# A decode step with attention and a Mish branch: dense input product in the first unit, division behind two key pieces, w2 in the key ring, output sum in four column groups

## Chip, cores and metric

The kernel runs on one core of one Trainium2 chip. The metric is the device time of one execution in microseconds (us). 1 MB is 10^6 bytes here.

## The reference

A decode step for two sequences: attention over the last 4096 positions of a long key/value cache, a dense branch with the Mish activation, and the input itself are added.

```python
def _A_ref(x, k_cache, v_cache, wq, wo):     # x (2, 1, 448)
    W = 4096                                  # of 32768 positions; Hq 16, Hkv 8, Dh 256
    q = (x @ wq).reshape(B, Sq, Hq, Dh).transpose(0, 2, 1, 3)
    k = repeat(k_cache[:, :, Sk - W:, :], 2, axis=1)
    v = repeat(v_cache[:, :, Sk - W:, :], 2, axis=1)
    p = softmax(einsum("bhqd,bhkd->bhqk", q, k) * Dh ** -0.5)
    o = einsum("bhqk,bhkd->bhqd", p, v)
    return o.transpose(0, 2, 1, 3).reshape(B, Sq, Hq * Dh) @ wo

def _B_ref(x, w1, b1, w2):                    # w1 (448, 1792), w2 (1792, 448)
    h = einsum("bsd,df->bsf", x, w1) + b1
    return einsum("bsf,fd->bsd", h * tanh(softplus(h)), w2)

xn = layernorm(x)
return x + _A_ref(xn, ...) + _B_ref(xn, ...)
```

All inputs are bf16. Keys and values of the window are 33.6 MB each, wq and wo 3.67 MB each, w1 and w2 1.606 MB each.

## The kernel before

The 16 pairs of batch and key head are worked in four units (U = 4) of four pairs. A unit reads its keys in four pieces and its values in four pieces of 2.097 MB each, every one a tile of 128 partitions by 16,384 bytes, and its rows of wo in two loads of 0.459 MB.

All large loads go out on SP's queue, in the order in which the program names them, and a load whose buffer is still in use holds up all loads behind it. The buffers are two rings: `k_pool` with three buffers for key pieces, and `v_pool` with four, in which value pieces, the two parts of wq, w1 and the three parts of w2 take turns. wo has two buffers. The order of the work on each engine is that of the program (`manual_schedule`).

A unit runs like this. `turn(u, r, i)` (L216) transposes half a key piece on VectorE into `kt[i]`; eight of them make a unit's keys. `scores(u, i)` forms a half of the scores on PE: one product with a mask (L273), then 128 products of 128x128 weights (L284), and ScalarE takes the exponential (L292). `weigh(u)` sums the exponentials with products by ones (L304), and VectorE reduces the sum (L312) and takes its reciprocal. `values(u, g)` makes 64 products with value piece g (L325). `finish(u)` divides by the sum on VectorE (L337). `mix(u)` multiplies by wo with eight products of 448 columns (L351), which add to `psA`, a 2x448 accumulator; it stands behind the next unit's `weigh`.

Around them, `project()` (L238) makes the queries behind the first two key pieces. `dense_in()` stands at the end of the first unit: 196 products (L376) with 64 columns of w1 each, in turn for the upper and the lower half of the output partitions, then the Mish operations on VectorE and ScalarE (L385 to L403). w1 itself is loaded (L364) behind the second key piece of unit 1. `dense_out(part)` (L418) adds the 14 products with w2 to `psA`, in parts of 8, 5 and 1; w2's loads (L411) stand behind the first values of the last unit. At the end VectorE copies `psA` (L470) and one DMA writes it out (L471).

```python
    for u in range(U):
        ...                                   # turns, project, loads of v
        values(u, 0) ... values(u, 2)
        if not last:
            load_k(u + 1, 0); load_k(u + 1, 1)
            if u == 0:
                load_w1()
            load_k(u + 1, 2); load_wo(u); load_k(u + 1, 3)
        values(u, 3)
        finish(u)
        if u == 0:
            dense_in()
    dense_out(0); mix(U - 1); dense_out(1); dense_out(2)
```

Of the kernel before, what the change touches and what calls it, by code (L numbers as in the profile page):

```python
# [17 lines left out]
def kernel(  # L18
# [13 lines left out]
    nc = tc.nc  # L32
# [23 lines left out]
    HW = HqDh // 2  # L56
    NCH = HW // P
    F2 = F // 2
    NI = F // P
    assert Sq == 1 and Bsz == 2 and rep == 2 and Dh == 256 and Hq == 16  # L60
    assert W == 4096 and D == 448 and F == 1792
    scale = float(Dh) ** -0.5

# [19 lines left out]
    def ring(name):  # L83
        return v_pool.tile([P, KE], BF16, tag="v", name=name)
# [3 lines left out]
    def load_k(u, r):  # L88
        t = k_pool.tile([P, KE], BF16, tag="k", name="k")
        src = kview[u][:, s0:, :].rearrange("j (c t) d -> c j (t d)", c=C)  # L90
        nc.sync.dma_start(out=t[:], in_=src[:, :, r * KE : (r + 1) * KE])  # L91
        k_t[u, r] = t

    def load_v(u, g):
        t = ring("v")
        src = vview[u][:, s0:, :].rearrange("j (g x t) d -> g x j (t d)", g=G, x=C)
        nc.sync.dma_start(out=t[:], in_=src[g])
        v_t[u, g] = t

    def load_wo(u):  # L100
        w = wo_pool.tile([P, KU, rep, 2 * D], BF16, tag="wo", name="wo")
# [81 lines left out]
    for odd in range(2):  # L183
# [12 lines left out]
    nc.tensor.matmul(  # L196
        psA[:, :],
        lhsT=ident[0:Bsz, 0:Bsz],
        rhs=x_bf[:],
        start=True,  # L200
        stop=False,
        skip_group_check=True,
    )

    kt = [
        kt_pool.tile([P, TH * NB, P // (R * J), R, J], FP32, name=f"kt{i}") for i in range(NH)
# [139 lines left out]
    def mix(u):  # L346
        oT, w = state.pop(("oT", u)), wo_t.pop(u)
        for k2 in range(KU):
            for h in range(rep):
                for c in range(2):  # L350
                    nc.tensor.matmul(  # L351
                        psA[:, :],
                        lhsT=oT[:, c, k2 * rep + h, :],
                        rhs=w[:, k2, h, c * D : (c + 1) * D],
                        start=False,
                        stop=False,
                        skip_group_check=True,
                    )

    act_bf = consts.tile([P, NI, Bsz], BF16)  # L360

    def load_w1():
        t = ring("w1")
        nc.sync.dma_start(  # L364
            out=t[:, 0 : NS * F2], in_=B_w1.flatten().rearrange("(p e) -> p e", p=P)
        )
        state["w1"] = t

    def dense_in():
        w1 = state.pop("w1")  # L370
        w1_v = w1[:, 0 : NS * F2].rearrange("p (s q i) -> p s i q", s=NS, i=NI)
        h_ps = ps_m.tile([P, NI, Bsz], FP32, tag="m", name="h_ps")
        for i in range(NI):
            for s in range(NS):
                for k in range(2):
                    nc.tensor.matmul(  # L376
                        h_ps[k * 64 : (k + 1) * 64, i, :],
                        lhsT=w1_v[:, s, i, :],
                        rhs=xs[:, s, k, :],
                        start=(s == 0),  # L380
                        stop=(s == NS - 1),
                        skip_group_check=True,
                    )
        h_sb = consts.tile([P, NI, Bsz], FP32, name="h_sb")
        nc.vector.tensor_tensor(  # L385
            out=h_sb[:],
            in0=h_ps[:],
            in1=b1_sb[:].unsqueeze(2).to_broadcast([P, NI, Bsz]),
            op=ALU.add,
        )  # L390
        u_sb = consts.tile([P, NI, Bsz], FP32, name="u_sb")
        nc.scalar.activation(out=u_sb[:], in_=h_sb[:], func=ACT.Exp)
        t_sb = consts.tile([P, NI, Bsz], FP32, name="t_sb")
# [3 lines left out]
        den = consts.tile([P, NI, Bsz], FP32, name="den_sb")  # L397
# [9 lines left out]
    def load_w2():  # L407
        w2_in = B_w2.flatten().rearrange("(p e) -> p e", p=P)
        for lo, hi in w2_parts:
            t = ring("w2")  # L410
            nc.sync.dma_start(out=t[:, 0 : (hi - lo) * D], in_=w2_in[:, lo * D : hi * D])  # L411
            state["w2", lo] = t

    def dense_out(part):
        lo, hi = w2_parts[part]
        t = state.pop(("w2", lo))
        for i in range(lo, hi):
            nc.tensor.matmul(  # L418
                psA[:, :],
                lhsT=act_bf[:, i, :],  # L420
                rhs=t[:, (i - lo) * D : (i - lo + 1) * D],
                start=False,
                stop=(i == NI - 1),
                skip_group_check=True,
            )

    for u in range(U):
        if u == 0:
            load_k(0, 3)
        for r in range(R):  # L430
            for i in range(NH):
                turn(u, r, i)
            if u == 0 and r == 1:
                project()
# [10 lines left out]
        load_v(u, 2)  # L445
        load_v(u, 3)
        values(u, 0)
        if last:
            load_w2()
        values(u, 1)  # L450
        values(u, 2)
        if not last:
            load_k(u + 1, 0)
            load_k(u + 1, 1)
            if u == 0:
                load_w1()
            load_k(u + 1, 2)
            load_wo(u)
            load_k(u + 1, 3)
        values(u, 3)  # L460
        finish(u)
        if u == 0:
            dense_in()
    dense_out(0)
    mix(U - 1)
    dense_out(1)
    dense_out(2)

    res = consts.tile([Bsz, D], BF16)
    nc.vector.tensor_copy(out=res[:], in_=psA[:, :])  # L470
    nc.sync.dma_start(out=out.flatten_outer_dims(), in_=res[:])  # L471


# [28 lines left out]
```

## Time and profile before

| what | value |
|---|---|
| median of 3 runs | 213.32 us (213.04 to 213.45) |
| profiled execution, its own time | 212.86 us |
| profiled execution, span from first to last instruction | 211.1 us |
| PE busy | 93.2 us (44% of the span) |
| VectorE (DVE) busy | 83.5 us (40%) |
| ScalarE (ACT) busy | 7.9 us (4%) |
| mean read rate over the span | 368 GB/s |
| DMA on the chain that ended last | 56% |

Times in the rows are microseconds from the span's first instruction. PE is TensorE's products, PEld its weight loads, DVE is VectorE, SPq the instructions of SP that issue DMAs. A name such as `kt<-k` is what an instruction writes and reads. An idle time in square brackets stands before the instruction, with what ended it. "issue" means that the engine waited for nothing that the profile shows. The granted clock is that of TensorE; 1.00 is 2.4 GHz and 0.50 is 1.2 GHz.

### The profile page before, as it was taken

Reading aid. Unit: us, or ns where it says so; the run is one execution under the profiler, and the core shown is the slowest. Engines: PE = TensorE matmul, PEld = TensorE weight load, DVE = VectorE, ACT = ScalarE, POOL = GpSimd, SP = SyncE. Lnnn points to the kernel's source line nnn. Section 1 sums busy time; section 2 is a strip of 40 time slices with the busy share of each in tenths; the row PEclk is TensorE's granted clock in tenths of the full one; section 3 lists DMA queues with packets and bytes.
Section 4 is the critical chain, followed back from the end, with each engine's and each line's share of the span. In section 5 each row is a group of like instructions: output and inputs, shape, how many; then the busy total and the mean of one; then the engine's idle time right before and its main releaser. Section 6 shows DMA issues by size and latency. Waiting matters only on the chain.

```text
span 211.1 us, 5109 instructions
## 1 busy us (share of the span) xinstructions
PE 93.2 (44%) x2434; PEld 76.3 (36%) x2434; DVE 83.5 (40%) x81; ACT 7.9 (4%) x12; POOL 2.7 (1%) x12
## 2 busy tenths in 40 slices
PE   0203402966304980008792400079952000959794
PEld 0103302856304970007572300066751000845741
DVE  5693369110000019994010698531003995501001
ACT  5000000110000000001100000011000000110000
POOL 5000000000000000000000000000000000000000
PEclk9999999985555555555695555557855555587559
DMA  5999999999999500899999999999999999999920
GB/s 215 432 425 428 435 422 432 428 422 422 432 414 437 220 0 0 335 416 435 435 418 422 435 395 438 435 416 425 432 419 422 409 419 411 438 419 419 333 90 2
DMA packets 7821, 78.00 MB, mean 370 GB/s; under 512 B 884, under 2 KB 3064, under 8 KB 3320
## 3 DMA queue, kind: packets, MB, share of 16 engines
q1 hardware_dynamic: 7652, 77.66, 88.0%
q8 instruction: 19, 0.31, 0.6%
q10 hardware_dynamic: 148, 0.01, 0.0%
q14 instruction: 2, 0.02, 0.0%
HBM read 77.67 MB, written 0.00 MB: 368 GB/s over the span
## 4 chain that ended last, share of the span: by engine, by line
DMA 56%; PE 22%; DVE 16%; issue 4%; ACT 1%; SPq 0%; ACTq 0%
DMA k<-in_A_k_cache_dram 19%; DMA wo<-in_A_wo_dram 15%; DVE kt L216 15%; DMA v<-in_A_v_cache_dram 13%; DMA w<-in_B_w_dram 9%; PE sc L284 7%; PE h_ps L376 6%; PE o L325 5%; PE psA L418 2%; PE psA L351 2%; ACT p L292 1%; PE dn L304 0%; PE sc L273 0%; DVE res L470 0%; SPq L91 0%
## 5 line engine op out<-in xcount | busy, mean ns | idle before, releaser
L216 DVE STREAM_TRANSPOSE kt<-k 128x2048 f32<-128x2048 f32 x32 | 71.3, 2282 | 9.8 <-DMA k<-in_A_k_cache_dram 9.8
L284 PE MATMUL sc<-qd,kt 128*128 128x32 bf16 x1024 | 29.0, 185 | 70.4 <-DVE kt L216 63.7
L284 PEld LDWEIGHTS <-kt 128*128 128x128 bf16 x1024 | 28.0, 102 | 73.9 <-DVE kt L216 65.7
L325 PE MATMUL o<-p,v 128*128 128x8 bf16 x1024 | 28.8, 167 | 14.6 <-issue 13.0
L325 PEld LDWEIGHTS <-v 128*128 128x128 bf16 x1024 | 27.8, 101 | 17.2 <-issue 15.4
L337 DVE TENSOR_TENSOR oT<-o,rec 128x16 bf16<-128x16 f32 x4 | 0.7, 175 | 46.2 <-PE o L325 46.2
L312 DVE TENSOR_REDUCE rec<-dn 128x8 f32<-128x512 f32 x4 | 2.8, 691 | 33.0 <-PE dn L304 33.0
L376 PE MATMUL h_ps<-xs,w 128*64 128x2 bf16 x196 | 11.6, 255 | 9.0 <-DMA w<-in_B_w_dram 9.0
L376 PEld LDWEIGHTS <-w 128*64 128x64 bf16 x196 | 11.5, 212 | 9.1 <-DMA w<-in_B_w_dram 9.1
L292 ACT ACTIVATE p<-sc 128x512 bf16<-128x512 f32 x8 | 4.8, 597 | 147.4 <-PE sc L284 147.4
L351 PE MATMUL psA<-wo,oT 128*2 128x448 bf16 x32 | 9.5, 452 | 0.2 <-issue 0.2
L238 PE MATMUL q_ps<-xs,wq 128*128 128x4 bf16 x112 | 3.3, 166 | 13.3 <-DMA wq<-in_A_wq_dram 13.3
L385 DVE TENSOR_TENSOR h_sb<-h_ps,b_sb 128x28 f32<-128x28 f32 x1 | 0.2, 189 | 20.4 <-PE h_ps L376 20.4
L238 PEld LDWEIGHTS <-wq 128*128 128x128 bf16 x112 | 3.1, 104 | 13.8 <-DMA wq<-in_A_wq_dram 13.8
L351 PEld LDWEIGHTS <-oT 128*2 128x2 bf16 x32 | 3.1, 103 | 9.3 <-issue 8.4
L273 PE MATMUL sc<-mneg,ident 128*128 128x512 bf16 x8 | 4.6, 575 | 0.0
L418 PE MATMUL psA<-w,act_bf 128*2 128x448 bf16 x14 | 4.4, 480 | 0.0
L304 PE MATMUL dn<-p,ones 128*128 128x512 bf16 x8 | 3.6, 455 | 1.8 <-ACT p L292 1.8
L179 PE MATMUL xr_ps<-ident,xrow 2*128 2x2 bf16 x7 | 1.0, 181 | 5.4 <-DVE xrow L178 5.4
L470 DVE CAST res<-psA 2x448 bf16<-2x448 f32 x1 | 0.6, 610 | 6.4 <-PE psA L418 6.4
L179 PEld LDWEIGHTS <-xrow 2*128 2x128 bf16 x7 | 0.7, 99 | 5.6 <-DVE xrow L178 5.4
L250 DVE CAST qT<-q_ps 128x16 bf16<-128x16 f32 x4 | 0.4, 167 | 5.6 <-PE q_ps L238 5.6
(39 smaller groups left out, 18.1 us busy)
## 6 DMA issues: line engine op xcount, KB each, us to landing
k<-in_A_k_cache_dram SPq DMA_DIRECT2D x16, 2048.0 KB, 25.0
v<-in_A_v_cache_dram SPq DMA_DIRECT2D x16, 2048.0 KB, 22.9
wo<-in_A_wo_dram SPq DMA_DIRECT2D x8, 448.0 KB, 30.8
wq<-in_A_wq_dram SPq DMA_DIRECT2D x1, 2048.0 KB, 16.2
w<-in_B_w_dram SPq DMA_DIRECT2D x1, 1568.0 KB, 18.7
wq<-in_A_wq_dram SPq DMA_DIRECT2D x1, 1536.0 KB, 19.2
w<-in_B_w_dram SPq DMA_DIRECT2D x1, 896.0 KB, 6.7
w<-in_B_w_dram SPq DMA_DIRECT2D x1, 560.0 KB, 6.5
```

What stands on the lines that cost most here:

```text
L179: nc.tensor.transpose(xr_ps[:, s, :], xrow[:].rearrange("b a o -> b (a o)"), ident[0:Bsz, 0:Bsz])
L216: nc.vector.transpose(out=kt[i][:, :, :, r, :], in_=t[:, i * w : (i + 1) * w].bitcast(FP32).rearrange("p (a c j) -> p a c j", c=P // (R * ...
L238: nc.tensor.matmul(q_ps[:, c, :, :].rearrange("p k b -> p (k b)"), lhsT=wq_t[s][:, c * P : (c + 1) * P], rhs=xs_m[s], start=(s == 0 and c ...
L273: nc.tensor.matmul(sc[:].rearrange("p t q -> p (t q)"), lhsT=ident[:], rhs=mneg[:].rearrange("p a j h -> p (a j h)"), start=True, stop=Fal ...
L284: nc.tensor.matmul(sc[:, t, :], lhsT=ktm[i][:, t, n, e, :], rhs=qd[:, u, 2 * n + e, :, :].rearrange("p g q -> p (g q)"), start=False, stop ...
L292: nc.scalar.activation(out=p_t[i][:].rearrange("p t g q -> p (t g q)"), in_=sc[:].rearrange("p t q -> p (t q)"), func=ACT.Exp, scale=scale,)
L304: nc.tensor.matmul(dn[:].rearrange("p a q -> p (a q)"), lhsT=ones[:], rhs=p_t[i][:].rearrange("p t g q -> p (t g q)"), start=(i == 0), sto ...
L312: nc.vector.tensor_reduce(out=rec[:], in_=dn[:].rearrange("p a q -> p q a"), axis=AXIS.X, op=ALU.add)
L325: nc.tensor.matmul(po[:, c, :], lhsT=vv[:, t, c, :], rhs=p_t[t // TH][:, t % TH, g, :], start=(g == 0 and t == 0 and c == 0), stop=(g == G ...
L351: nc.tensor.matmul(psA[:, :], lhsT=oT[:, c, k2 * rep + h, :], rhs=w[:, k2, h, c * D : (c + 1) * D], start=False, stop=False, skip_group_ch ...
L376: nc.tensor.matmul(h_ps[k * 64 : (k + 1) * 64, i, :], lhsT=w1_v[:, s, i, :], rhs=xs[:, s, k, :], start=(s == 0), stop=(s == NS - 1), skip_ ...
L418: nc.tensor.matmul(psA[:, :], lhsT=act_bf[:, i, :], rhs=t[:, (i - lo) * D : (i - lo + 1) * D], start=False, stop=(i == NI - 1), skip_group ...
```

## The change

Four things are changed together.

- `dense_in` moves into the first unit, behind `project` and the third key piece's turns; w1 is loaded ahead of the first unit's fourth key piece. w1, b1 and w2 are laid out in two halves, so that `dense_in` is 49 products with 128 columns of w1 and 4 moving columns. The Mish operations become `mish()`, behind the fourth piece's turns.
- `finish(u)`, the division, stands behind the turns of the next unit's first two key pieces. The loads of a unit all stand ahead of its scores.
- w2 goes into one buffer of the key ring, in three loads: its first half behind v(3,1), and five and two blocks of its second half behind the last value piece. The last value piece comes in two loads, of 24 and 8 positions of 32. `dense_out(0)` stands ahead of the last `values`.
- The accumulator `acc` is 128x112: the 448 output columns are cut into four groups, each at another 32 partitions, so every product of 448 columns becomes four of 112 (`add_rows`). The copy at the end is 128x112, and two DMAs on two queues write the result.

```diff
-    NI = F // P
+    NI = F2 // P
+    DG = D // G
...
-    def load_v(u, g):
-        t = ring("v")
+    def load_v(u, g, lo=0, hi=T):
+        if lo == 0:
+            v_t[u, g] = ring("v")
+        t = v_t[u, g]
...
-    b1_sb = consts.tile([P, NI], BF16)
-    nc.scalar.dma_start(out=b1_sb[:, :], in_=B_b1.rearrange("(q c) -> q c", q=P))
+    b1_sb = consts.tile([P, 2, NI], BF16)
+    nc.scalar.dma_start(out=b1_sb[:], in_=B_b1.rearrange("(k q c) -> q k c", k=2, q=P))
...
-    psA = ps_a.tile([Bsz, D], FP32)
...
+    acc = ps_a.tile([P, DG], FP32)
+    for g in range(G):
+        nc.tensor.matmul(
+            acc[32 * g : 32 * (g + 1), :],
+            lhsT=ident[0:Bsz, 0:32],
+            rhs=x_bf[:, g * DG : (g + 1) * DG],
...
+    def add_rows(lhsT, rows, stop=False):
+        for g in range(G):
+            nc.tensor.matmul(
+                acc[32 * g : 32 * g + Bsz, :],
+                lhsT=lhsT,
+                rhs=rows[:, g * DG : (g + 1) * DG],
+                start=False,
+                stop=stop,
+                skip_group_check=True,
+            )
...
         for i in range(NI):
             for s in range(NS):
-                for k in range(2):
-                    nc.tensor.matmul(
-                        h_ps[k * 64 : (k + 1) * 64, i, :],
-                        lhsT=w1_v[:, s, i, :],
-                        rhs=xs[:, s, k, :],
...
+                nc.tensor.matmul(
+                    h_ps[:, i, :, :].rearrange("p k b -> p (k b)"),
+                    lhsT=w1_v[:, s, i, :],
+                    rhs=xs_m[s],
...
-    w2_parts = [(0, 8), (8, 13), (13, NI)]
...
+    w2_parts = ((0, 0, NI), (1, 0, 5), (1, 5, NI))
+
+    def load_w2(part):
+        if part == 0:
+            state["w2"] = k_pool.tile([P, KE], BF16, tag="k", name="w2")
...
+    load_w1()
+    load_k(0, 3)
+    turns(0, 0)
+    turns(0, 1)
+    project()
+    turns(0, 2)
+    dense_in()
+    turns(0, 3)
+    mish()
     for u in range(U):
...
         last = u == U - 1
         if last:
             load_wo(u)
         load_v(u, 0)
         load_v(u, 1)
+        if last:
+            load_w2(0)
+        load_v(u, 2)
+        if last:
+            load_v(u, 3, 0, 24)
+            load_v(u, 3, 24, T)
+            load_w2(1)
+            load_w2(2)
+        else:
+            load_v(u, 3)
+            load_k(u + 1, 0)
+            load_k(u + 1, 1)
+            load_k(u + 1, 2)
+            load_wo(u)
+            load_k(u + 1, 3)
         scores(u, 0)
         scores(u, 1)
         weigh(u)
         if u > 0:
             mix(u - 1)
...
+        for g in range(G):
+            if last and g == G - 1:
+                dense_out(0)
+            values(u, g)
         if not last:
...
+            turns(u + 1, 0)
+            turns(u + 1, 1)
+            finish(u)
+            turns(u + 1, 2)
+            turns(u + 1, 3)
+    finish(U - 1)
     mix(U - 1)
     dense_out(1)
     dense_out(2)
...
+    res = consts.tile([P, DG], BF16)
+    nc.vector.tensor_copy(out=res[:], in_=acc[:])
...
+    nc.sync.dma_start(out=out_v[0], in_=res_v[0])
+    nc.scalar.dma_start(out=out_v[1], in_=res_v[1])
```

## Rows read from the trace of the kernel before

**Rows 1.** The page: GB/s in 40 equal slices, bytes read, instruction fetches.
```profile
GB/s 215 432 425 428 435 422 432 428 422 422 432 414 437 220 0 0 335 416 435 435 418 422 435 395 438 435 416 425 432 419 422 409 419 411 438 419 419 333 90 2
...
q8 instruction: 19, 0.31, 0.6%
...
HBM read 77.67 MB, written 0.00 MB: 368 GB/s over the span
```

**Rows 2.** SP's timeline: start us, us, engine, line, load, count.
```profile
48.76 1.10 SPq L104 DMA_DIRECT2D wo<-in_A_wo_dram  x2
84.08 0.54 SPq L91 DMA_DIRECT2D k<-in_A_k_cache_dram  x1
...
194.89 3.65 SPq L411 DMA_DIRECT2D w<-in_B_w_dram  x3
```

**Rows 3.** The chain that ended last: start us, us, what.
```profile
47.57 18.71 DMA w<-in_B_w_dram
...
66.32 11.61 PE h_ps L376 x196
...
79.64 15.39 DVE kt L216 x7
```

**Rows 4.** VectorE's timeline: start us, us, operation, count, idle time and its end.
```profile
8.48 4.50 DVE L216 STREAM_TRANSPOSE kt<-k 128x2048 f32<-128x2048 f32 x2 [1.46 <-DMA k<-in_A_k_cache_dram]
...
28.21 4.50 DVE L216 STREAM_TRANSPOSE kt<-k 128x2048 f32<-128x2048 f32 x2 [2.16 <-DMA k<-in_A_k_cache_dram]
33.11 4.51 DVE L216 STREAM_TRANSPOSE kt<-k 128x2048 f32<-128x2048 f32 x2 [0.39 <-DMA k<-in_A_k_cache_dram]
...
127.17 4.50 DVE L216 STREAM_TRANSPOSE kt<-k 128x2048 f32<-128x2048 f32 x2 [0.28 <-DMA k<-in_A_k_cache_dram]
...
177.56 4.51 DVE L216 STREAM_TRANSPOSE kt<-k 128x2048 f32<-128x2048 f32 x2 [2.46 <-DMA k<-in_A_k_cache_dram]
190.42 0.69 DVE L312 TENSOR_REDUCE rec<-dn 128x8 f32<-128x512 f32 x1 [8.36 <-PE dn L304]
```

**Rows 5.** PE's timeline: values of unit 2, and the last values and sums.
```profile
155.59 3.58 PE L325 MATMUL o<-p,v 128*128 128x8 bf16 x128 [2.51 <-issue]
161.51 0.19 PE L325 MATMUL o<-p,v 128*128 128x8 bf16 x1 [2.35 <-issue]
...
199.51 1.52 PE L325 MATMUL o<-p,v 128*128 128x8 bf16 x51 [1.34 <-DMA v<-in_A_v_cache_dram]
...
201.67 3.15 PE L418 MATMUL psA<-w,act_bf 128*2 128x448 bf16 x8
204.61 2.56 PE L351 MATMUL psA<-wo,oT 128*2 128x448 bf16 x8
207.00 1.30 PE L418 MATMUL psA<-w,act_bf 128*2 128x448 bf16 x6
```

**Rows 6.** The timeline of all engines from 206 us on: copy and output.
```profile
208.34 0.61 DVE L470 CAST res<-psA 2x448 bf16<-2x448 f32 x1 [6.41 <-PE psA L418]
208.98 0.33 SPq L471 DMA_DIRECT2D out_dram<-res  x1
```

**Rows 7.** Groups by line and shape: busy us, mean ns of one, idle before.
```profile
L325 PE MATMUL o<-p,v 128*128 128x8 bf16 x1024 | 28.8, 167 | 14.6 <-issue 13.0 <-DMA v<-in_A_v_cache_dram 1.5
...
L325 PEld LDWEIGHTS <-v 128*128 128x128 bf16 x1024 | 27.8, 101 | 17.2 <-issue 15.4 <-DMA v<-in_A_v_cache_dram 1.7
L376 PE MATMUL h_ps<-xs,w 128*64 128x2 bf16 x196 | 11.6, 255 | 9.0 <-DMA w<-in_B_w_dram 9.0
...
L264 DVE CAST qd<-qr_ps 32x256 bf16<-32x256 f32 x4 | 1.7, 420 | 0.5 <-PE qr_ps L254 0.5
...
L250 DVE CAST qT<-q_ps 128x16 bf16<-128x16 f32 x4 | 0.4, 167 | 5.6 <-PE q_ps L238 5.6
```

**Rows 8.** Busy times and granted clock in two stretches of the last sums.
```profile
201.70:204.60 2.90, 2.90 (x9) 0.95 (x9) 0.17 (x1) 0.00 (x0) 0.00 (x0) 0.50 0.14 47
206.50:208.30 1.80, 1.80 (x10) 0.61 (x8) 0.00 (x0) 0.00 (x0) 0.00 (x0) 1.00 0.00 0
```

More of the change, by code (lines that the diff above doesn't have):

```diff
@@ L58 @@
     F2 = F // 2
-    NI = F // P
-    assert Sq == 1 and Bsz == 2 and rep == 2 and Dh == 256 and Hq == 16
+    NI = F2 // P
+    DG = D // G
+    assert Sq == 1 and Bsz == 2 and rep == 2 and Dh == 256 and G * DG == D and Hq == 16
     assert W == 4096 and D == 448 and F == 1792
@@ L92, in load_k @@
         k_t[u, r] = t
-    def load_v(u, g):
-        t = ring("v")
+    def load_v(u, g, lo=0, hi=T):
+        if lo == 0:
+            v_t[u, g] = ring("v")
+        t = v_t[u, g]
         src = vview[u][:, s0:, :].rearrange("j (g x t) d -> g x j (t d)", g=G, x=C)
-        nc.sync.dma_start(out=t[:], in_=src[g])
-        v_t[u, g] = t
+        nc.sync.dma_start(
+            out=t[:, lo * Dh : hi * Dh], in_=src[g, :, :, lo * Dh : hi * Dh]
+        )
     def load_wo(u):
@@ L193 @@
     xs_m = [xs[:, s, :, :].rearrange("p a b -> p (a b)") for s in range(NS)]
-    psA = ps_a.tile([Bsz, D], FP32)
-    nc.tensor.matmul(
[L197 to L203, printed above, removed]
+    acc = ps_a.tile([P, DG], FP32)
[4 more added lines that the diff above has]
+            rhs=x_bf[:, g * DG : (g + 1) * DG],
+            start=True,
+            stop=False,
+            skip_group_check=True,
+        )
+    def add_rows(lhsT, rows, stop=False):
[6 more added lines that the diff above has]
+                stop=stop,
+                skip_group_check=True,
+            )
     kt = [
@@ L350, in mix @@
                 for c in range(2):
[L351 to L360, printed above, removed]
+                    add_rows(oT[:, c, k2 * rep + h, :], w[:, k2, h, c * D : (c + 1) * D])
+    act_bf = consts.tile([P, NI, 2, Bsz], BF16)
     def load_w1():
@@ L371, in dense_in, with mish @@
         w1_v = w1[:, 0 : NS * F2].rearrange("p (s q i) -> p s i q", s=NS, i=NI)
-        h_ps = ps_m.tile([P, NI, Bsz], FP32, tag="m", name="h_ps")
+        h_ps = ps_m.tile([P, NI, 2, Bsz], FP32, tag="m", name="h_ps")
         for i in range(NI):
             for s in range(NS):
-                for k in range(2):
-                    nc.tensor.matmul(
-                        h_ps[k * 64 : (k + 1) * 64, i, :],
-                        lhsT=w1_v[:, s, i, :],
-                        rhs=xs[:, s, k, :],
[L380 to L384, printed above, removed]
+                nc.tensor.matmul(
+                    h_ps[:, i, :, :].rearrange("p k b -> p (k b)"),
+                    lhsT=w1_v[:, s, i, :],
+                    rhs=xs_m[s],
+                    start=(s == 0),
+                    stop=(s == NS - 1),
+                    skip_group_check=True,
+                )
+        state["h"] = h_ps
+    def mish():
+        h_ps = state.pop("h")
+        shape = [P, NI, 2, Bsz]
+        h_sb = consts.tile(shape, FP32, name="h_sb")
         nc.vector.tensor_tensor(
@@ L387, in dense_in @@
             in0=h_ps[:],
-            in1=b1_sb[:].unsqueeze(2).to_broadcast([P, NI, Bsz]),
+            in1=b1_sb[:].rearrange("p k i -> p i k").unsqueeze(3).to_broadcast(shape),
             op=ALU.add,
         )
-        u_sb = consts.tile([P, NI, Bsz], FP32, name="u_sb")
+        u_sb = consts.tile(shape, FP32, name="u_sb")
         nc.scalar.activation(out=u_sb[:], in_=h_sb[:], func=ACT.Exp)
-        t_sb = consts.tile([P, NI, Bsz], FP32, name="t_sb")
+        t_sb = consts.tile(shape, FP32, name="t_sb")
         nc.vector.scalar_tensor_tensor(
@@ L396, in dense_in @@
         )
-        den = consts.tile([P, NI, Bsz], FP32, name="den_sb")
+        den = consts.tile(shape, FP32, name="den_sb")
         nc.vector.tensor_scalar(
@@ L403, in dense_in, with turns @@
         nc.vector.tensor_tensor(out=act_bf[:], in0=h_sb[:], in1=t_sb[:], op=ALU.mult)
-    w2_parts = [(0, 8), (8, 13), (13, NI)]
[L407 to L412, printed above, removed]
+    w2_parts = ((0, 0, NI), (1, 0, 5), (1, 5, NI))
+    def load_w2(part):
+        if part == 0:
+            state["w2"] = k_pool.tile([P, KE], BF16, tag="k", name="w2")
+        k, lo, hi = w2_parts[part]
+        w2_in = B_w2.flatten().rearrange("(k p e) -> k p e", k=2, p=P)
+        at = k * NI * D
+        nc.sync.dma_start(
+            out=state["w2"][:, at + lo * D : at + hi * D],
+            in_=w2_in[k, :, lo * D : hi * D],
+        )
     def dense_out(part):
-        lo, hi = w2_parts[part]
-        t = state.pop(("w2", lo))
+        k, lo, hi = w2_parts[part]
         for i in range(lo, hi):
[L418 to L424, printed above, removed]
-            )
-    for u in range(U):
[L428 to L434, printed above, removed]
+            at = (k * NI + i) * D
+            add_rows(
+                act_bf[:, i, k, :], state["w2"][:, at : at + D], stop=(k == 1 and i == NI - 1)
+            )
+    def turns(u, r):
+        for i in range(NH):
+            turn(u, r, i)
+    load_w1()
[7 more added lines that the diff above has]
+    mish()
+    for u in range(U):
         last = u == U - 1
@@ L467 @@
     dense_out(2)
-    res = consts.tile([Bsz, D], BF16)
-    nc.vector.tensor_copy(out=res[:], in_=psA[:, :])
-    nc.sync.dma_start(out=out.flatten_outer_dims(), in_=res[:])
+    res = consts.tile([P, DG], BF16)
+    nc.vector.tensor_copy(out=res[:], in_=acc[:])
+    out_v = out.flatten_outer_dims().rearrange("b (g c) -> b g c", g=G)
+    res_v = res[:].rearrange("(g r) c -> r g c", g=G)
+    nc.sync.dma_start(out=out_v[0], in_=res_v[0])
+    nc.scalar.dma_start(out=out_v[1], in_=res_v[1])
 _INS = ['A_x', 'A_k_cache', 'A_v_cache', 'A_wq', 'A_wo', 'B_x', 'B_w1', 'B_b1', 'B_w2']
```

19 lines of the change are left out of this document (removed).

## The prediction

> **What bounds the kernel now.** I read the slices of the page first, because a decode step that has 77.67 MB to read can end no earlier than its reads. The DMA rate stands near 425 GB/s in nearly every slice and falls in two places only: slices 13 to 16 (220, 0, 0, 335 GB/s) and the last three [rows 1]. The first hole, counted against 425 GB/s, is (205 + 425 + 425 + 90)/425 = 2.7 slices of 5.28 us, 14 us. The SP timeline tells why the queue ran dry: after w1 (L364), one key piece (L91) and the wo pieces (L104) were issued from 47.57 to 49.9 us, the next load, again L91, goes out at 84.08 [rows 2, 3]. The chain of waits fills in the rest: dense_in (L376) runs on PE from 66.32 for 11.61 us as soon as w1 is there, the Mish operations follow it on VectorE, and only then, at 79.64, the seven transposes that were queued behind them [rows 3]. The load at 84.08 wanted the buffer of the piece that the first two of these turn (2 x 2.2 us = 4.4).
>
> The second place is the end. Landings can be read off the rows in which an engine's idle time ended with a DMA: the first piece at 8.48, w1 at 66.32, the last key piece at 177.56, the last value piece at 199.51 [rows 3 to 5]. After that w2 (1.606 MB) still has to come, 1.606/0.427 = 3.8 us, to about 203.3; PE works until 208.3, the copy takes 0.61, and the output leaves at 208.98 [rows 5, 6].
>
> **The stream's own rate.** From 8.48 to 66.32 us there landed k, wq, k, k, four v, two k, w1: 9 x 2.097 + 3.670 + 1.606 = 24.15 MB in 57.84 us, 417.5 GB/s. From 127.17 to 199.51 there landed 13 pieces of 2.097 and six wo pieces of 0.459 MB, 30.02 MB in 72.34 us, 415 GB/s [rows 3 to 5]. Together 416. The stretch with the fewest breaks, 33.11 to 66.32 (14.19 MB), gives 427. I take 416: an unbroken stream of 181 us has the small breaks of both stretches.
>
> **The change part by part.** *w1 and dense_in in the first unit.* w1 is issued ahead of the fourth key piece, in a third buffer of the v ring that waits for nothing; the loads behind it on SP land 1.606/0.427 = 3.8 us later, and are themselves no shorter or longer. dense_in goes from 196 products of 64 columns (11.6 us, 59 ns each [rows 3]) to 49 of 128. A full load and product of 128x128 takes 28.8/1024 = 28 ns [rows 7]; the columns here lie 7 elements apart, so I bound it by 28 and 2 x 59 ns: 1.4 to 5.8 us. It starts when w1 lands, about 28.2 + 3.8 = 32 us by the first unit's third key piece, and the next thing PE has is the scores after a key piece that lands near 37: hidden either way. On SP the load of v(0,3) waits for it, until 34 to 38, with k and three v, 8.4 MB or 20 us, still queued. The Mish operations come after all transposes of the first unit, where VectorE waited 8 us for PE anyway (as before the reduce at 190.42 [rows 4]). Cost zero; the hole goes.
>
> *Is there a new hole?* The tightest wait left on SP is the same one as before: the fourth key piece of the next unit needs its first one turned. When that first one has landed, two key pieces and two wo pieces are still queued: 5.11 MB, 12.3 us, against two transposes of 2.25 us [rows 4]. 7.8 us of cover remain. The other loads wait for values or turns of a piece that landed at least two loads earlier. So the last byte lands at 8.48 + (77.67 - 2.10)/0.416 = 190.1 us, instead of 203.3. With 427 it would be 185.5.
>
> *Division behind two key pieces.* Four transposes (9 us) go ahead of it on VectorE. Who waits: the next mix and the next unit's first values, both behind the next unit's scores, over 10 us later. In the last unit nothing is put ahead of it. Zero; it keeps the turns, and so SP's key loads, from waiting for values(u, 3).
>
> *w2 in the key ring, last v piece cut in two.* Before, its three loads waited for values of the last unit (194.89 on [rows 2]); now they wait for turns that end some 20 us before the queue reaches them. Counting back from 190.1 at 416 GB/s: last v part 188.2, its first 24 rows 186.9, v(3,2) 183.1, last key piece 163.9. The b1 load, 256 short runs instead of 128, lies ahead of ScalarE's first table load; what follows from that on VectorE ended 1.46 us before the first key piece was there [rows 4]: zero.
>
> *Sum in four column groups.* Each of 448 columns becomes four of 112. The old one paces at (204.61 - 201.67)/8 = 0.37 us at a granted clock of 0.50, 1.2 GHz, and at most 1.30/6 = 0.22 at 1.00, 2.4 GHz [rows 5, 8]. Nothing in the trace runs four column groups. From below: four issues at 28 ns, 0.11 us. From above: the same columns one after the other, 0.37. Beyond that, rival 2. I take 0.125, since at 1.2 GHz 112 columns are a quarter of 0.37, 0.09, which hides under the four issues, and since L376 already changes between two column halves with every product at 59 ns spacing with 255 ns each, so several are in flight [rows 3, 7]. For the same thing the Trainium skill (TensorE: Matmul & The Clock Gate, Part 3: Packing small matmuls) gives 2.38 times for three column tiles; by that a set would be about 0.37/2.38 = 0.155 us, an estimate, and my sum 0.45 us later. No run here shows it yet.
>
> **The sum, in the span of the profiled run.** Key piece 163.9. From the last key landing to the end of the second dn product took 177.56 to 190.4 = 12.8 before, where the reduce follows at once [rows 4], with one instruction-fetch gap in it: 176.7. mix(2), eight sets, 1.0: 177.7. values(3,0) and (3,1), 128 products at 28 ns: 181.3. There a second gap of about 2.4 us is likely: PE's instructions come in 19 packets of 16 KB [rows 1], 128 products each, and under a full DMA queue a run of products goes 128 per 5.9 us (155.59 to 161.51, gaps of 2.4) [rows 5]. v(3,2) lands at 183.1, so values(3,2) end at 185 to 186, dense_out(0) (seven sets, 0.9) at 186 to 186.8. Then PE waits for data: last v part 188.2, 16 products 0.45, division with its hand-overs 0.25, mix(3) 1.0, five sets 0.65, and the last two after 190.1: 190.8. The copy is of 128x112 instead of 2x448; rows of 16 and 256 elements take 167 and 420 ns, so about 0.27 [rows 7]: 191.1. From the old copy's end, 208.95, to the end of the span 2.14 [rows 6], and the two output DMAs go out side by side on SP and ScalarE: 193.2, against 211.1. The profiled run took 212.86, 1.76 more than its span: 195.0. It lies 0.46 under the median of 213.32, so I predict 195.5.
>
> **The rivals.** *1. Groups run one after the other.* Then a set costs 0.37 as now. mix(2) +2.0 and dense_out(0) +1.7 come ahead of the last v part and eat the spare 0.1 to 0.9 us of PE; after it come 64 products of values(3,3) that no longer hid, 1.8, mix(3) 3.0, seven sets 2.6. End of PE 195.0 to 198.0, as far as the fetch gap hides under the longer sets; time 199.7 to 202.7. For it: no row shows overlap of long products. Against: the spacing of L376. Chance 0.17.
>
> *2. Slower: changing the column group stops the array.* If a product in another group may start only when the one before is out, each of the 28 + 60 in the tail and the 32 of mix(2) costs its own duration instead of 0.03 us. By L376 that is 0.255 for 2 columns, with 110 more at 1.2 GHz 0.34; 120 x 0.31 = 37 us, time about 232. It turns the sign from (211.1 - 193.2)/120 + 0.03 = 0.18 us a product on. Against it: L376 changes halves at 59 ns, and the weight loads of L325, all on 128 rows, add up to 1024 x 101 ns = 103 us in 27.8 us of busy time, under running products [rows 7]. Chance 0.04. The Trainium skill speaks for this one (same page, Part 3, The mechanism): weight loads overlap running products only where the row groups differ, and all four groups here use all rows. By that rule the time would be that of this rival; the trace disagrees for whole-array loads, as just said, and does not show it for groups of 32.
>
> *3. The pieces of a tile wait for each other.* If dense_out(0) waits for all three w2 loads, which are parts of one tile, then 190.1 + 0.9 + 1.8 + 0.25 + 1.0 + 0.9 = 195, time 199.7. Against: the second wo load into one tile went out with the first, two in 1.10 us [rows 2]. With it I count a hole that merely moves. Together 0.08.
>
> *4. Faster:* the stream keeps 427 and PE keeps up: 190.8 to 192.5. 0.06.
>
> **How the numbers follow.** My forecast, 193 to 198, has 0.65. With rival 1, most of 3 and the edge of 4 the range 192.5 to 202.5 holds a little over 8 in 10; its lower end is the faster rate, its upper end rival 1. Faster than 213.32 by over 0.2%, about what a measurement of this kernel can tell from no change, are all but rival 2 and the worst of 3: 0.95; same 0.01; slower 0.04.
>
> **What would show it.** No slice under 400 GB/s between the first and the last two; no L91 issue that comes after its queue has emptied; last key piece turned from about 164; v(3,3)'s products waiting for DMA, not issue; a set of four at 0.11 to 0.16 us. It is wrong if PE has no wait for v in the last unit (then instruction fetch or the groups bind), if a set takes 0.3 or more, or if a new stretch without data appears.

## The result and the profile after

| | before | after |
|---|---|---|
| median | 213.18 us | 198.03 us (197.72 to 198.26) |
| ratio to before, 95% interval | | 0.929 (0.927 to 0.932) |
| profiled execution | 212.86 us | 197.72 us |
| its span | 211.1 us | 195.2 us |

The forecast was 195.5 us, in a range of 192.5 to 202.5. The page of the changed kernel: the span, the read rate in 40 slices (of 4.88 us now) and the packets in which instructions were fetched.

```profile
span 195.2 us, 5096 instructions
...
GB/s 215 396 427 425 434 430 429 430 430 423 423 423 430 423 408 430 430 423 426 426 423 426 396 433 426 426 426 430 426 423 420 397 421 421 430 416 420 394 140 2
...
q8 instruction: 18, 0.29, 0.6%
```

The slices of 220, 0, 0 and 335 GB/s [rows 1] have no counterpart. From the second slice to the 38th the rate never falls under 394. The forecast had named 400 as the mark; four slices lie between 394 and 397, none of them a stretch without data. The median lies 0.03 us above the band of 193 to 198 that the forecast put first.

SP's timeline, start us, us, line, load, count. The last of these loads stood 84 us into the old run [rows 2].

```profile
35.57 6.55 SPq L92 DMA_DIRECT2D k<-in_A_k_cache_dram  x3
42.18 1.10 SPq L108 DMA_DIRECT2D wo<-in_A_wo_dram  x2
66.04 0.54 SPq L92 DMA_DIRECT2D k<-in_A_k_cache_dram  x1
```

The fourth key load of unit 1 now goes out at 66.04, some 7.7 us before the queue would be empty. VectorE's timeline (idle time and what ended it in brackets) shows the landings of the last unit's key piece and of one in mid-run.

```profile
103.28 4.50 DVE L232 STREAM_TRANSPOSE kt<-k 128x2048 f32<-128x2048 f32 x2 [11.17 <-DMA k<-in_A_k_cache_dram]
109.46 4.50 DVE L232 STREAM_TRANSPOSE kt<-k 128x2048 f32<-128x2048 f32 x2 [1.67 <-DMA k<-in_A_k_cache_dram]
114.45 4.51 DVE L232 STREAM_TRANSPOSE kt<-k 128x2048 f32<-128x2048 f32 x2 [0.43 <-DMA k<-in_A_k_cache_dram]
...
163.26 4.50 DVE L232 STREAM_TRANSPOSE kt<-k 128x2048 f32<-128x2048 f32 x2 [2.84 <-DMA k<-in_A_k_cache_dram]
```

VectorE waits for keys before every pair of transposes; before, it worked through a backlog. The last key piece is there at 163.26, 14.3 us earlier than at 177.56 [rows 4].

PE's timeline of the first dense product and of the end. L212 is the sum in four groups, L341 values, L300 scores.

```profile
32.18 2.77 PE L384 MATMUL h_ps<-xs,w 128*128 128x4 bf16 x49 [7.67 <-DMA w<-in_B_w_dram]
...
173.56 1.04 PE L300 MATMUL sc<-qd,kt 128*128 128x32 bf16 x35 [1.68 <-issue]
...
175.65 0.56 PE L212 MATMUL acc<-wo,oT 128*2 128x112 bf16 x32
176.15 1.63 PE L341 MATMUL o<-p,v 128*128 128x8 bf16 x59
179.75 2.00 PE L341 MATMUL o<-p,v 128*128 128x8 bf16 x69 [1.98 <-issue]
182.46 1.73 PE L341 MATMUL o<-p,v 128*128 128x8 bf16 x59 [0.70 <-DMA v<-in_A_v_cache_dram]
185.95 0.30 PE L341 MATMUL o<-p,v 128*128 128x8 bf16 x5 [1.76 <-issue]
186.18 0.82 PE L212 MATMUL acc<-w,act_bf 128*2 128x112 bf16 x28
187.41 1.87 PE L341 MATMUL o<-p,v 128*128 128x8 bf16 x64 [0.41 <-DMA v<-in_A_v_cache_dram]
189.55 1.20 PE L212 MATMUL acc<-wo,oT 128*2 128x112 bf16 x32 [0.27 <-DVE oT L353]
190.50 0.90 PE L212 MATMUL acc<-w,act_bf 128*2 128x112 bf16 x28
```

From the last key piece on, PE stops for "issue" after every 128 products (35 + 2 + 32 + 59, then 69 + 59), three times some 1.8 us, and twice for a value piece. The trace has the starts of the instruction packets, too: 171.12, 177.37 and 183.54 us. PE goes on 2.4 us after each, at 173.56, 179.75 and 185.95, so these stops are waits for instructions. The end, all engines:

```profile
191.44 0.28 DVE L494 CAST res<-acc 128x112 bf16<-128x112 f32 x1 [1.95 <-PE acc L212]
191.74 0.67 SPq L497 DMA_DIRECT2D out_dram<-res  x1
191.75 0.58 ACTq L498 DMA_DIRECT2D out_dram<-res  x1
```

From the copy's end at 191.72 to the end of the span it is 3.5 us; before it was 2.1 [rows 6].

### The profile page after: what moved, and what is told of

It is laid out like the page before. It is cut to its first block, busy times and chain, and to the rows that moved or that the text cites. A ratio compares the mean times of both kernels' runs of the same rounds, so it can differ in the third digit from the quotient of the medians.

```text
span 195.2 us, 5096 instructions
## 1 busy us (share of the span) xinstructions
PE 74.0 (38%) x2426; PEld 66.2 (34%) x2428; DVE 83.8 (43%) x81; ACT 7.9 (4%) x12; POOL 2.7 (1%) x12
## 4 chain that ended last, share of the span: by engine, by line
DMA 86%; DVE 8%; PE 2%; issue 1%; SPq 1%
DMA k<-in_A_k_cache_dram 55%; DMA wo<-in_A_wo_dram 16%; DMA v<-in_A_v_cache_dram 15%; DVE kt L232 8%; PE o L341 1%; PE acc L212 1%; SPq L108 0%; SPq L92 0%; DVE res L494 0%; DVE oT L353 0%; SPq L100 0%
## 5 line engine op out<-in xcount | busy, mean ns | idle before, releaser
L232 DVE STREAM_TRANSPOSE kt<-k 128x2048 f32<-128x2048 f32 x32 | 72.1, 2290 | 53.1 <-DMA k<-in_A_k_cache_dram 53.1
L300 PE MATMUL sc<-qd,kt 128*128 128x32 bf16 x1024 | 28.7, 184 | 67.7 <-DVE kt L232 62.0
L300 PEld LDWEIGHTS <-kt 128*128 128x128 bf16 x1024 | 27.7, 102 | 70.3 <-DVE kt L232 63.6
L341 PE MATMUL o<-p,v 128*128 128x8 bf16 x1024 | 29.2, 168 | 19.2 <-issue 18.1
L341 PEld LDWEIGHTS <-v 128*128 128x128 bf16 x1024 | 28.1, 103 | 21.5 <-issue 19.7
L384 PE MATMUL h_ps<-xs,w 128*128 128x4 bf16 x49 | 2.8, 193 | 7.7 <-DMA w<-in_B_w_dram 7.7
L384 PEld LDWEIGHTS <-w 128*128 128x128 bf16 x49 | 2.7, 152 | 7.8 <-DMA w<-in_B_w_dram 7.8
L289 PE MATMUL sc<-mneg,ident 128*128 128x512 bf16 x6 | 3.2, 537 | 0.0
L212 PE MATMUL acc<-wo,oT 128*2 128x112 bf16 x128 | 2.9, 232 | 0.3 <-DVE oT L353 0.3
L212 PEld LDWEIGHTS <-oT 128*2 128x2 bf16 x128 | 1.9, 90 | 3.1 <-issue 2.8
L280 DVE CAST qd<-qr_ps 32x256 bf16<-32x256 f32 x4 | 1.7, 420 | 0.5 <-PE qr_ps L270 0.5
L212 PE MATMUL acc<-w,act_bf 128*2 128x112 bf16 x56 | 1.7, 292 | 0.0
```

The source lines that it names most:

```text
L212: nc.tensor.matmul(acc[32 * g : 32 * g + Bsz, :], lhsT=lhsT, rhs=rows[:, g * DG : (g + 1) * DG], start=False, stop=stop, skip_group_check= ...
L232: nc.vector.transpose(out=kt[i][:, :, :, r, :], in_=t[:, i * w : (i + 1) * w].bitcast(FP32).rearrange("p (a c j) -> p a c j", c=P // (R * ...
L280: nc.vector.tensor_copy(out=qd[rows, :, :, g, :], in_=qr_ps[rows].rearrange("p n u q -> p u n q"),)
L289: nc.tensor.matmul(sc[:].rearrange("p t q -> p (t q)"), lhsT=ident[:], rhs=mneg[:].rearrange("p a j h -> p (a j h)"), start=True, stop=Fal ...
L300: nc.tensor.matmul(sc[:, t, :], lhsT=ktm[i][:, t, n, e, :], rhs=qd[:, u, 2 * n + e, :, :].rearrange("p g q -> p (g q)"), start=False, stop ...
L341: nc.tensor.matmul(po[:, c, :], lhsT=vv[:, t, c, :], rhs=p_t[t // TH][:, t % TH, g, :], start=(g == 0 and t == 0 and c == 0), stop=(g == G ...
```

## Experiments: where the gain comes from

The kernel before ran beside each group of runs; its median went from 212.71 to 213.57 us. A difference of some 0.5 us between a run and the changed kernel is therefore not told apart here.

**1. The first part alone.** The kernel before; `mish` is the part of `dense_in` from L384 on.

```diff
+            load_w1()
             load_k(0, 3)
...
+            if u == 0 and r == 2:
+                dense_in()
+        if u == 0:
+            mish()
...
-            if u == 0:
-                load_w1()
...
-        if u == 0:
-            dense_in()
```

> The kernel before with one part of the change alone: w1 is loaded ahead of the fourth key piece, dense_in (still 196 products of 64 columns) stands behind the third key piece's turns, and the Mish operations behind the first unit's last turns. Theory (the hole came from VectorE's transposes, and with them SP's next key load, standing behind Mish, dense_in and w1): the hole closes, the last key piece lands near 164, and from there it takes the 33.5 us of the kernel before (177.6 to 211.1) to the end: span 197 to 198, time 199 to 200.5. Rival (the division ahead of the turns, or the loads behind values, open the hole anew): time over 203, with slices under 350 GB/s in mid-run.

200.14 us (199.42 to 200.53), 12.9 under the kernel before beside it. Its read rate, and VectorE's timeline where the dip is:

```profile
GB/s 212 416 435 432 445 422 426 422 419 422 439 429 422 404 275 422 432 445 425 417 422 429 396 445 425 422 422 425 435 425 415 390 421 429 429 425 401 310 68 2
```
```profile
67.03 0.17 DVE L337 TENSOR_TENSOR oT<-o,rec 128x16 bf16<-128x16 f32 x1 [10.98 <-PE o L325]
67.12 17.65 DVE L216 STREAM_TRANSPOSE kt<-k 128x2048 f32<-128x2048 f32 x8
...
165.06 4.51 DVE L216 STREAM_TRANSPOSE kt<-k 128x2048 f32<-128x2048 f32 x2 [1.47 <-DMA k<-in_A_k_cache_dram]
```

The hole is closed but for one slice of 275: 196 products delay the first values, the division waits for them until 67.0, and the transposes behind it for that. The last key piece is turned from 165.06, and 33.6 us later the span ends, as before. The first part carries 12.9 of the 15.1 us.

**2. w1 late, but 49 products; and 3. Mish behind the turns as well.** Both from the changed kernel.

```diff
-    load_w1()
     load_k(0, 3)
...
     turns(0, 2)
-    dense_in()
     turns(0, 3)
-    mish()
...
             load_k(u + 1, 1)
+            if u == 0:
+                load_w1()
...
+        if u == 0:
+            dense_in()
+            mish()          # run 3: behind turns(u + 1, 3) instead
         if not last:
             turns(u + 1, 0)
```

> The changed kernel with w1's load and dense_in back where they were (w1 behind the second key piece of unit 1, dense_in and Mish behind the first unit's values), but with 49 products. Theory (the hole is as long as w1's landing, the products, Mish and two transposes together reach beyond the end of the queue): 66.3 + 2.8 + 1.6 + 4.5 = 75 us for the next key load instead of 84, the queue runs dry at about 73.4, and the restart takes 2 us: a hole of 3 to 4 us, time 201 to 202.5. Rival (the place of w1 makes the hole, whatever the number of products): a hole of 11 to 14 us, time 209 to 212.

203.16 us (202.65 to 203.38).

```profile
GB/s 219 406 429 426 441 422 425 432 425 425 425 427 424 407 126 278 441 428 415 425 445 422 415 415 432 425 415 422 445 418 418 403 424 421 423 416 427 404 123 2
```
```profile
75.30 0.54 SPq L92 DMA_DIRECT2D k<-in_A_k_cache_dram  x1
```

The load goes out at 75.30, as worked out; the hole, (299 + 147)/425 slices of 5.01 us, is 5.3 us. The hole is 1.3 us longer than the 3 to 4 that were expected, the mechanism as stated: of the old 14 us, some 9 were the 196 products (11.6 us against 2.8).

> As the run with w1 late and 49 products, but Mish stands behind all turns of unit 1 on VectorE. Theory (VectorE's order alone makes the hole): no slice under 390 GB/s, time 197.5 to 198.7, as the changed kernel. Rival (dense_in in mid-run holds up PE or the v ring enough to open a hole): a hole of 2 us or more, time 200 or more.

198.37 us (198.26 to 198.45), no slice under 398 between the second and the 37th, and the load that went out at 75.30 goes out at 62.40:

```profile
GB/s 215 399 429 423 448 422 428 428 422 422 428 425 418 427 408 428 428 422 425 425 422 425 398 439 422 428 425 428 428 422 425 400 410 429 428 412 432 371 114 2
```
```profile
62.40 0.54 SPq L92 DMA_DIRECT2D k<-in_A_k_cache_dram  x1
```

So neither w1's place nor dense_in's in mid-run matters by itself: what made the hole is that VectorE's transposes, and through their buffers SP's next load, stood behind operations that waited for w1.

**4. One group.** `add_rows` is one product of 448 columns into a 2x448 `psA`, with one copy and one DMA, as before.

> The changed kernel with the output sum as it was: products of 448 columns into a 2x448 accumulator, one copy, one output DMA. Theory (the four groups run side by side, and the sums behind the last value piece are on the path): 15 sets at 0.37 instead of about 0.14 us add 3.5, the copy adds 0.3, the single output DMA gives back 1.3 to 2: time 199.5 to 201. Rival (the sums hide behind the last w2 bytes, the groups give nothing): only the output's gain shows, time 196 to 197.

199.72 us (198.89 to 201.09). PE's last rows:

```profile
188.42 2.04 PE L339 MATMUL o<-p,v 128*128 128x8 bf16 x64
190.73 3.15 PE L210 MATMUL psA<-wo,oT 128*2 128x448 bf16 x8 [0.27 <-DVE oT L351]
193.67 1.68 PE L210 MATMUL psA<-w,act_bf 128*2 128x448 bf16 x7
```

The copy and the output:

```profile
195.39 0.61 DVE L492 CAST res<-psA 2x448 bf16<-2x448 f32 x1 [4.71 <-PE psA L210]
196.03 0.32 SPq L493 DMA_DIRECT2D out_dram<-res  x1
```

In the profiled run PE ends 3.9 us later than with four groups, the copy is 0.3 longer, the output 0.9 shorter, and outside the span 0.7 less is spent (below). These are the 2.7 us between the profiled 200.41 and 197.72; in the medians the groups, with the output that goes with them, gain 1.7 net. The four runs lie far apart, from 198.89 to 201.09, so the size of this gain is known to about 1 us only. The groups are the one part besides the first that shows.

**5. Division ahead of the turns** (`finish(u)` moved up two lines).

> The changed kernel with the division of a unit ahead of the next unit's transposes, as before. Theory (values(u, 3) end at 61.3 us in the first unit and the next key piece lands at 61.5, so the division holds up no transpose for long): no slice under 390 GB/s in mid-run, time within 0.5 us of the changed kernel, 197.6 to 198.5. Rival (the transposes, and with them the fourth key load of a unit, fall back to the end of values and the queue runs short, as in the run of the kernel before with w1 early, where one slice fell to 275 GB/s): a slice under 350, time 199 or more.

198.19 us (197.81 to 198.71), no slice under 393 up to the 37th. Worth nothing here. Run 1, where the division stood behind 196 products, is the case in which its place could count; the two were not tried together.

**6. w2 in the value ring, last piece uncut**, `dense_out(0)` behind the last values.

> The changed kernel with w2 back in the value ring, behind an uncut last value piece, and dense_out(0) behind the last values. Theory (w2's loads wait for values of the last unit but go out before the queue is empty; only 28 products and the uncut piece come onto the path): 0.3 to 0.9 us more, time 198.3 to 199.0. Rival (the third w2 load, which waits for values(3,2) at 186, leaves the queue empty): 2 us or more, time 200 and up.

197.61 us (197.39 to 197.88): not slower, against the theory. SP issues w2 between 179.80 and 186.3, before the queue is empty, and PE's end is no later:

```profile
186.49 1.87 PE L341 MATMUL o<-p,v 128*128 128x8 bf16 x64 [0.52 <-DMA v<-in_A_v_cache_dram]
188.40 0.82 PE L212 MATMUL acc<-w,act_bf 128*2 128x112 bf16 x28
```

With w2's first half behind it, the whole value piece is there at 186.5, where the changed kernel's first 24 rows came at 187.4. So its 64 products start 0.9 us earlier, and the 28 products, some 0.6 to 0.8 us, come behind them: the two about cancel, and PE ends at 191.12 instead of 191.40.

## Experiments: what sets the end

**7. Fewer instructions.** Leaves out 192 products, three value pieces of the first unit (`if u > 0 or g == 0` ahead of `values(u, g)`).

> The changed kernel without the 192 products of values(0,1) to values(0,3): the attention of the first unit then lacks three quarters of its values; every load stays. The trace shows the instruction-fetch packets of 16 KB, one per 128 products, and a landing that takes 1.3 us longer than its bytes beside the 1st, 9th and 17th of them (the last is at 183.5 us, beside the first part of the last value piece). Theory (each packet holds back one DMA engine's share of the stream, in turns of eight): with 1.5 segments fewer the 17th comes after the last byte, the last value part lands 1.2 to 1.4 us earlier, time 196.4 to 197.0. Rival (the stream's own rate drifts, fetches have no part): time 197.7 to 198.4.

197.84 us (197.60 to 198.08). The stream did as the theory said. Of the 12,288-byte rows of the last value piece (1536 KB, us from issue to landing) the first line is the changed kernel's, the second this run's; both were issued at 158.36.

```profile
v<-in_A_v_cache_dram SPq DMA_DIRECT2D x1, 1536.0 KB, 29.0
```
```profile
v<-in_A_v_cache_dram SPq DMA_DIRECT2D x1, 1536.0 KB, 27.6
```

1.4 us earlier, and so is what follows it. But the time did not move, since PE has now another boundary in its way:

```profile
184.26 2.00 PE L341 MATMUL o<-p,v 128*128 128x8 bf16 x69 [2.60 <-issue]
186.19 0.82 PE L212 MATMUL acc<-w,act_bf 128*2 128x112 bf16 x28
186.95 0.99 PE L341 MATMUL o<-p,v 128*128 128x8 bf16 x31
189.08 1.04 PE L341 MATMUL o<-p,v 128*128 128x8 bf16 x33 [1.15 <-issue]
```

No wait for v is left in the last unit: instruction supply bounds PE's end there. Stream and supply bound the end side by side, and taking 1.4 us from one shows the other. The 192 products that are left out also move the boundaries, so the two were not varied apart.

**8. One output DMA from a gathered tile** (four copies by VectorE into 2x448).

> The changed kernel, but VectorE copies the four column groups into one 2x448 tile with four copies, and one DMA on SP writes it, as in the kernel before. Theory (the two output DMAs of four short pieces each cost 1.3 us more from the copy's end to the end of the span, and 0.7 us after it): four copies add 0.5 to 0.8, the rest falls back to the 2.1 and 1.8 us of the kernel before: time 196.3 to 197.2. Rival (the end of the span is set by something else, such as ScalarE's part in the last barrier): 198.3 to 198.8.

198.24 us (197.85 to 198.47). The copies take what the single DMA gives back:

```profile
191.92 1.16 DVE L495 CAST res<-acc 2x112 bf16<-2x112 f32 x4 [2.45 <-PE acc L212]
193.11 0.33 SPq L498 DMA_DIRECT2D out_dram<-res  x1
```

From the copies' start to the end of the span 3.8 us, as with two DMAs (191.44 to 195.2). And 2.7 us still lie outside the span: the output is not what lengthens that. From the copies' end it is 2.6 us, as in run 4, whose copy and single DMA are those of the kernel before, and not the 2.1 that were expected. So of the 1.4 us by which the changed kernel's end is longer, 0.9 goes with the two DMAs and 0.5 with something else in it. That 0.5 lies behind the output's last packet: from there to the closing instructions the trace has 0.8 us before and 1.3 in runs 4, 8 and 12. Its cause stays open. One DMA straight from the 128x112 tile was not measured, so what the second queue costs and what the short pieces cost is not told apart.

**9. Loads in another order** (`load_wo(u)` behind `load_k(u + 1, 3)`; all of w2 behind the last value piece, `dense_out(0)` behind `mix(3)`).

> The changed kernel with two changes of order in the loads: wo of a unit behind the next unit's fourth key piece, so that the last key piece lands 2.2 us earlier, and all of w2 behind the last value piece, with dense_out(0) behind mix(3). Theory (behind the last value part 188.6 us PE needs 2.8 us, the stream only 1.8; with 0.8 MB of w2 moved behind it the value part lands 1.9 us earlier and PE waits for the last bytes): PE ends 0.5 to 0.8 us earlier, time 197.1 to 197.6. Rival (PE's instruction fetches, 128 products per 6 us from the last key piece on, set the end): no gain or less than 0.3, time 197.7 to 198.3.

196.92 us (196.42 to 197.90), a gain of 1.1, but not by the theory. In its profile PE ends at 191.3 as before, stopped between two products of dense_out:

```profile
188.29 0.82 PE L212 MATMUL acc<-w,act_bf 128*2 128x112 bf16 x27
190.16 1.12 PE L212 MATMUL acc<-w,act_bf 128*2 128x112 bf16 x29 [1.05 <-issue]
```

The span is 0.1 to 0.9 us shorter over its runs (194.6 to 195.1 against 195.2 to 195.5); the rest is outside the span, 1.8 instead of 2.5 in the profiled run; of the six runs five have 1.8 to 2.1 there, and one, the slowest, 2.8.

**10. 63 products done twice in the first unit, loads in the kernel's own order.** `for i in [*range(NI), 0, 1, *range(NI)]` in `dense_in`.

> The changed kernel, with the loads in its own order, and 63 products of dense_in done twice in the first unit: nothing is moved but the boundaries between PE's instruction packets, the last of which then falls among the last values products instead of 29 products before the end. Theory (2.5 to 2.7 us outside the span belong to a last packet that is fetched after the end): no packet behind the end of the span, 1.8 us outside the span, 0.7 to 0.9 less than the changed kernel; inside the span the packet that is now due among the last values products may cost up to 0.7. Rival (the late packet is harmless and the outside time has another cause, such as the order of the loads): 2.5 to 2.7 us outside the span.

199.16 us (199.04 to 199.42). The theory held outside the span. Inside, the packet cost 2.0 us where at most 0.7 was expected, so the time rose by 1.1 us, where a fall of 0.7 to 0.9 was forecast. Outside the span lie 1.8 us (199.04 - 197.3), and all 19 packets lie inside it:

```profile
q8 instruction: 19, 0.31, 0.6%
```

Inside, the boundary now stands among the last values products:

```profile
187.35 1.01 PE L341 MATMUL o<-p,v 128*128 128x8 bf16 x32
190.56 1.01 PE L341 MATMUL o<-p,v 128*128 128x8 bf16 x32 [2.19 <-issue]
```

The stop is 2.19 us there, and the span is 2 us longer. 63 products more at a place where PE has nothing to do, 160 us from the end, cost 1.1 us by where they push a boundary.

**11. Order and repeated products together; 12. copies on two engines as well.**

> As the run with the loads in another order, with 63 products of dense_in done twice in the first unit, where PE waits for keys: every later boundary between two instruction packets then falls 63 products earlier. In all runs so far 2.5 to 2.7 us lie outside the span where PE crosses such a boundary in its last 40 products or so within the last microsecond, and a packet comes 6 us later, behind the end; 1.8 us where it does not. Theory (the late packet costs the time): no packet behind the span's end, 1.8 us outside the span, time 0.6 to 0.9 less than the run without the repeated products. Rival (something else in the kernels with two output DMAs makes the difference): no change within 0.3 us.

197.13 us (196.96 to 197.47), no gain over run 9, which had lost the late packet already.

> As the run with 63 repeated products, and the four column groups are copied into one 2x448 tile, two groups by VectorE and two by ScalarE, and written by one DMA. With four copies on VectorE alone they took 1.16 us, and the one DMA landed 1.15 us after its issue instead of 1.98. Theory (two engines halve the copies): 0.3 to 0.6 us less than with two output DMAs. Rival (ScalarE loads a function table for the copy, 1.28 us in this trace, or waits for VectorE's reading of the same bank): 0.5 us or more longer.

196.23 us (195.82 to 196.52), ratio 0.920 (0.917 to 0.923) to before: the best of all, 1.8 us under the changed kernel by the medians, and its interval lies clear of the changed kernel's.

```profile
191.44 0.56 DVE L494 CAST res<-acc 2x112 bf16<-2x112 f32 x2 [2.31 <-PE acc L212]
191.47 0.52 ACT L494 CAST res<-acc 2x112 bf16<-2x112 f32 x2 [18.31 <-PE acc L212]
192.08 0.33 SPq L495 DMA_DIRECT2D out_dram<-res  x1
```

No table is loaded for ScalarE's copies; the output goes out at 192.08 instead of 193.11 (run 8). Against run 11 the medians fall by 0.9 us, where 0.3 to 0.6 was expected.

## Why the prediction was right, and where it was short

*What bounds the kernel.* Right. Run 1 and run 3 show the hole and its chain as read: VectorE's order, then SP's.

*The stream's rate.* Right. 416 GB/s gave the last byte at 190.1; it lands at about 190.5, an estimate: the w2 load before it landed 25.7 us after its issue at 164.40, at 190.1, and the last 0.23 MB take 0.5 us more. The last key piece was put at 163.9 and is turned at 163.26, the last v part's first 24 rows at 186.9 and come at 187.4.

*w1 and dense_in, zero cost.* Right: 2.77 us for 49 products, hidden from 32.18 to 35. *Tightest wait.* 7.8 us of cover worked out; the load goes out at 66.04, and two key pieces and wo, 12.3 us by their bytes, were queued from 61.5: some 7.7 remain.

*Division, and w2 in the key ring.* Division zero: right by run 5. Of the w2 part I had said only what it unblocks; by run 6 it is worth nothing that shows, since in the old place the loads, too, go out before the queue is dry.

*Four groups.* The mechanism was right, the size wrong: most sets (four products, one in each group) cost less than my lower bound of 0.11 us. Two stretches of the changed kernel (columns: stretch, us, PE, PEld, DVE, ACT, POOL busy, granted clock, DMA share, GB/s):

```profile
175.65:176.15 0.50, 0.50 (x34) 0.40 (x33) 0.39 (x1) 0.00 (x0) 0.00 (x0) 1.00 0.83 352
...
190.50:191.40 0.90, 0.90 (x29) 0.64 (x29) 0.00 (x0) 0.00 (x0) 0.00 (x0) 0.50 0.00 0
```

At 2.4 GHz 32 products take 0.50 us, 16 ns each, a set 0.063; at 1.2 GHz 28 products start over about 0.62 us (0.90 less the last one's run of 0.28), 23 ns each, a set 0.09, which is a quarter of the 0.37 of one product of 448 columns [rows 5, 8]. So four groups run side by side. They are not always as cheap: in run 6 the eight sets of mix(2), all at 1.2 GHz, take 0.85 us up to the first values product, 0.11 a set. The 28 ns that I took as the floor is the pace of whole-array weights of 128 columns; weights of 2 columns are not held to it. The factor of 2.38 that the Trainium skill (TensorE: Matmul & The Clock Gate, Part 3: Packing small matmuls) measured for three column tiles, by which a set would take 0.155 us, an estimate, lies under what four groups show here. Its rule that weight loads overlap running products only where row groups differ, which spoke for rival 2, does not hold for these groups of one set of rows: products start 16 to 23 ns apart.

*PE's chain.* I counted one fetch gap beyond the one within the scores, and there were two, 1.98 and 1.76 us. The last key piece 0.6 us early and the cheap sets of mix(2) made up for a part of it, and dense_out(0) ended at 187.0, 0.2 past the late end of what I gave. PE then waited 0.41 us for the last value piece, whose first 24 rows came at 187.4 instead of 186.9; from there PE ran its 64 products without a stop, to 189.28, where I had put 188.65. In mix(3) a third gap, of 0.3 us, took back what the cheaper sets gave. So PE's end came at 191.40 instead of 190.8.

*The end of the run*, which holds the larger miss. The step "to the end of the span 2.14, and the two output DMAs go out side by side" was mis-sized: it measured 3.5, 1.4 more. By runs 4 and 8, 0.9 of this goes with the two DMAs (0.3 of it is the longer issue, 0.67 instead of 0.33) and 0.5 has another cause, which is open. And I carried over 1.76 us outside the span; it was 2.5. With the 0.6 of PE these are 2.7 us, the whole difference between 195.0 and the profiled 197.72.

*Rivals.* None of the four occurred. Rival 1, groups one after the other, was priced at 199.7 to 202.7; run 4, where a set is one product of 448 columns, took 199.72 with the cheaper output. Against rival 3, dense_out(0) ran at 186.18, before the other w2 parts had landed.

*Luck.* The forecast of 195.5 was 2.5 us too low, and 198.03 lies just above the band of 193 to 198. It is inside the stated range only because that was held open up to 202.5 for rivals 1 and 3; the terms that were missed, the output and the time outside the span, had no part in it.

## To carry to other kernels

Before you shorten a transfer or a product, follow what is queued behind it on each engine: here an engine that was idle most of the time held up the load queue because a step that waited stood ahead of work that did not. An edit that moves work in mid-run is priced by the queue that is left when the moved wait ends, bytes over rate; under that, the length of the work is free. When a stream is made gapless, the next bounds lie in the tail and are small, so price every step after the last byte on its own, down to the output.

## What the runs showed of the hardware

- PE's instructions come in packets of 16 KB, 128 products each. In the changed kernel PE stops twelve times at such a boundary, for 1.3 to 3.0 us, where it runs product after product, and each stop ends 2.4 to 2.6 us after a packet has started. 63 products more in an idle time moved a boundary and with it 2.0 us of the span (run 10).
- In the changed kernel, a landing takes some 1.3 us more than its bytes beside the 1st, 9th and 17th packet: 103.28 to 109.46 is 6.2 us for a piece that else takes 4.9. With the 17th behind the last value piece, its first 24 rows landed 1.4 us earlier (run 7; in run 4, too, 27.5 us after issue instead of 29.0). In the kernel before it is the 1st, 7th and 15th packet (6.3 us from one landing to the next beside the 7th, 6.5 beside the 15th). That the packets go to eight DMA engines in turn is argued from these counts, of which the first in the kernel before, six, does not fit; the trace doesn't name the engine.
- In the kernels with 2.5 to 2.7 us outside the span (after, runs 2, 3, 5, 6, 8) the trace of the profiled run has a packet that starts 1.7 to 2.0 us behind the end of the span; in those with 1.8 (before, runs 1, 4, 7, 9 to 12) it has none. Run 10 changed only the boundaries and went from one to the other. What the end waits for there is open.
- 128x128 weights whose columns lie 14 bytes apart paced at 2.77/49 = 57 ns a product, against 28 for values, whose columns lie 4 bytes apart [rows 7]. The clock isn't the reason: the 49 ran at 2.4 GHz. The step alone was not varied.
